# The first chunk's k is turned on TensorE instead of loaded; every piece is issued in a new order

## The chip, the cores and the metric

One core of a Trainium2 chip runs the whole program. The metric is the device time of one execution in microseconds (us), the median over several runs. Two versions of this kernel can be told apart by measurement when they differ by some 0.2%, which is about 0.4 us here.

## The reference

Attention with a per-head decay, in blocks of 64 positions with a running state, followed by a gated convolution layer. Sizes: 4 batches, 8 heads, 768 positions, head size 64, model width 512.

```python
for b in range(nb):                              # nb = 768 / 64
    intra = einsum('bhic,bhjc->bhij', qb, kb) * Dmask          # lam ** (i - j), lower triangle
    intra = einsum('bhij,bhjd->bhid', intra, vb)
    inter = einsum('bhid,bhde->bhie', qb * lam_pow, kv_state)
    out[:, :, sl] = intra + inter
    kb_dec = kb * rev_pow                                      # lam ** (63 - j), for each row of k
    kv_state = lam_block * kv_state + einsum('bhsd,bhse->bhde', kb_dec, vb)
# x = out as (batch, position, 512)
gate = sigmoid(causal convolution of x with 5 taps per column)
return (gate * (x @ w_val)) @ w_out
```

## The kernel before, in words

Two batches are worked on at a time (`b` = 0, 1), and their 768 positions are cut into six chunks of 128. That makes twelve chunks, numbered 0 to 11. Chunks 0, 1 and 2 are "big": their scores are 128x128 per head. The others use two blocks of 64. Every chunk has two loads on the sync engine's DMA queue (SP): `ld.i.0` brings q and k transposed (`qT`, `kT`, head size on the partitions, batch 0 on partitions 0 to 63 and batch 1 on 64 to 127), and `ld.i.2` brings v and k with positions on the partitions. Each load is 1024 KB. So k comes twice: `kT` serves the scores, k itself serves the state.

The work is cut into named pieces, each on one engine. For chunk i:

- `s.i.u` (TensorE, L460 for big chunks): scores of four heads from kT and qT. Matmuls of fp32 show up as two records each, so `s.0.0` is 8 matmuls and 16 records.
- `m.i.b.u` (VectorE, L483): scores times the decay mask, out of PSUM into the tile `A`.
- `ia.i.u` (TensorE, L525): A times v, into the PSUM tile `xp`. There is one such tile (`"xp": 1` in `SLOTS`, two banks), so every holder of it waits until all readers of the one before are done.
- `kd.i` (ScalarE L401 or GpSimd L404): k times the decay of each row, in place in the loaded tile. `K_ACT` lists the chunks for which ScalarE does it, with one instruction per head, 8 in all.
- `st.i` (TensorE, L564): the state's outer product of scaled k and v. `up.i.0` (VectorE) adds it to the state. `in.i.0` (TensorE, L536) is q times the state, with `qd.i.u` (GpSimd) having scaled q before.
- `x.i`, `xh.i`, `xl.i`: the chunk's result out of `xp`, as a whole (ScalarE, L634), and split in a high and a low part. For chunks 0 and 1 (`X_DVE`) `xh` (ScalarE, L664) and `xl` (VectorE, L672) read `xp` themselves.
- `v.i.f` (TensorE, L732): one quarter of x @ w_val from three products of high and low parts, 12 matmuls. `p.*` (TensorE, L841) is the product with w_out.
- `t.*` (convolution taps, one on ScalarE and four on VectorE), `sg.*`, `ap.*`, `hh.*`, `hl.*`: the gate and its product with the value.

The weights arrive as raw 64-bit floats (`wv.0`, `wv.1`, `wo.0`, `wo.1`, each 1024 KB) and are turned into high and low 32-bit parts in quarters: `e` and `n` (VectorE, L261 and L268), `r` and `m` (ScalarE, L273 and L278), `s`, `w`, `v` (VectorE, L281, L287, L293), `h` (ScalarE, L299) and `l` (GpSimd, L303).

At the start TensorE is warmed with nine matmuls of zeros (`WARM`, L188), and one more dummy matmul, `f.0` (L206), is placed by the order.

The order is written out by hand in the string `ORDER`: pieces are issued one after the other as listed, with the buffers they take behind a colon, and every engine works off its own pieces in that order. Synchronisation is added by the framework, which keeps engines apart by whole PSUM banks. Before the change, TensorE's pieces begin `s.0.0 s.0.1 ia.0.0 ia.0.1 f.0 st.0 s.1.0 s.1.1 v.0.0 ia.1.0 ia.1.1 in.1.0 st.1 s.2.0`, and VectorE's begin with the two mask-making pieces `dm.0 dm.1` (L216), then `m.0.0.0 m.0.1.0 m.0.0.1 m.0.1.1`, `e n` of the first quarter, `e` of the second, `s w v` of the first, `xl.0 up.0.0 m.1.1.0 m.1.0.0 m.1.0.1 m.1.1.1`.

Of the kernel before, what the change touches and what calls it, by code (L numbers as in the profile page):

```python
# [37 lines left out]
wv.0.1.w wv.0.1.v wv.0.1.h ld.3.2:lv1 wv.1.0.n s.2.0:s0 wv.1.1.e:val3 s.2.1:u1,u2 up.1.0 xh.1 wv.0.1.l v.0.1
m.2.0.0:A0 m.2.1.0 wv.1.0.m:u0 xl.1 wv.1.0.w wv.1.0.r hi.0 pb.0.0:val0 m.2.0.1:A1 wv.1.0.s cv.e qd.2.0:qd1 wv.1.0.v
qd.2.1 wv.1.1.n x.1 wv.1.1.r cv.r s.4.0:s0 cv.n v.1.0:u3 v.1.1 wv.1.0.h wv.1.1.s wv.1.1.m:u0 m.2.1.1 wv.1.1.w wv.1.1.v  # L40
ia.2.0:xp0 ia.2.1 wv.1.0.l cv.m m.4.1.0:A0 kd.2.0 wv.1.1.h fd.1.0 wo.0.0.n:val1 cv.s in.2.0 x.2:x1 pb.1.0:val2
wv.1.1.l m.4.0.0 st.2:u1 wo.0.0.e wo.0.0.r up.2.0 qd.4.0:qd0 cv.w cv.v xh.2:xs1 wo.1.1.e:val3 t.0.0.0:u2,g0 s.3.0:s0
xl.2.0 wo.0.0.m:u0 v.0.2:u3 m.3.0.0:A1 ld.6.2:lv2 v.0.3 pb.0.1 t.0.0.1 kd.3.0 t.0.0.2 xl.2.1 t.0.0.3 wo.0.0.w qd.4.1
ld.5.0:lq2 wo.0.0.s t.0.0.4 v.1.2:u1 sg.0.0 qd.3.1:qd1 v.1.3 v.2.2:u3 v.2.3 pb.1.1 wo.1.1.n fd.2.0 wo.0.0.v m.3.1.0
wo.1.1.m:u2 wo.1.1.r ld.6.0:lq0 st.3:u0,u1 wo.0.0.h qd.3.0 ia.3.0:xp0 in.3.0 wo.1.1.w wo.1.1.s wo.1.1.v wo.0.0.l hi.1
s.5.0:s0 kd.4.0 v.2.0:u2 up.3.0 in.3.1 wo.0.1.e:val1 wo.0.1.r fd.3.0 wo.1.1.h wo.0.1.n wo.0.1.m:u0 wo.0.1.s wo.1.1.l
up.3.1 fd.3.1 ia.3.1 v.2.1 x.3 xh.3 xl.3.1 ia.4.0:xp0 t.0.1.0:u1 ld.5.2:lv1 wo.0.1.w xl.3.0 pb.2.0:val3 m.5.1.0:A1
# [81 lines left out]
def decay_attention_then_gated_conv(  # L129
# [193 lines left out]

    def plan_load(i):
        pair, c = divmod(i, NC)
        lds[i] = {}
        for lo, tag in ((0, "lq"), (2, "lv")):
# [575 lines left out]
```

## Time and profile before

| what | us |
|---|---|
| median of 3 runs (206.31 to 206.44) | 206.38 |
| the profiled execution's own time | 206.52 |
| its span (first to last instruction) | 204.7 |
| VectorE busy | 154.1 (75%) |
| ScalarE busy | 114.3 (56%) |
| GpSimd busy | 115.4 (56%) |
| chain that ended last, share of TensorE | 87% |
| chain that ended last, share of DMA | 9% |

Times within a profile count from the span's start. A timeline row gives start, duration, engine, line, operation, output<-inputs, shape, and in brackets the idle time of the engine ahead of it and what ended that idle time. PE is TensorE's matmul stream, PEld its weight loads, DVE VectorE, ACT ScalarE, POOL GpSimd, SPq the issue of DMAs. A merged row of several instructions gives the time from the first start to the last end.

### The profile page before, as it was taken

What the parts mean: (1) busy time and instruction counts of PE and PEld (TensorE: products, weight loads), DVE (VectorE), ACT (ScalarE), POOL (GpSimd) and SP (SyncE); (2) the same over time, 40 slices, a digit from 0 to 9 for tenths busy, and PEclk for the clock granted to TensorE, in tenths of its full rate; (3) what the DMA queues carried; (4) which work ended last, traced back from release to release, by engine and by line L of the source; (5) the groups of instructions that cost most, each with busy time, mean ns of one, the idle gap of its engine ahead of it and who ended that gap; (6) DMA issues with size and microseconds to landing.
All of it is one profiled execution on the core that took longest, in us unless ns stands there. A gap on an engine that the chain in (4) does not pass through costs nothing.

```text
span 204.7 us, 7451 instructions
## 1 busy us (share of the span) xinstructions
PE 197.6 (97%) x3312; PEld 171.6 (84%) x3312; DVE 154.1 (75%) x240; ACT 114.3 (56%) x218; POOL 115.4 (56%) x113
## 2 busy tenths in 40 slices
PE   7789899999999999999999999999999999999994
PEld 7668899999899988899888888888878888888883
DVE  5778999998969987998979996582668499853200
ACT  2079589797975788646484665233636255423131
POOL 5446457897897499919919995893686100000000
PEclk9999999999999999999999999999999999999999
DMA  5999999981528004950890693004020002210232
GB/s 175 426 429 419 422 424 423 421 360 27 195 51 362 8 3 118 373 232 3 297 297 29 203 400 122 3 3 152 8 106 0 0 3 102 102 51 14 93 127 78
DMA packets 7952, 36.15 MB, mean 177 GB/s; under 512 B 1136, under 2 KB 1392, under 8 KB 4336
## 3 DMA queue, kind: packets, MB, share of 16 engines
q1 hardware_dynamic: 7920, 35.68, 45.2%
q8 instruction: 26, 0.43, 0.9%
q14 instruction: 6, 0.05, 0.1%
HBM read 29.38 MB, written 6.29 MB: 174 GB/s over the span
## 4 chain that ended last, share of the span: by engine, by line
PE 87%; DMA 9%; SPq 2%; issue 0%; ACT 0%; ACTq 0%
PE op L841 33%; PE vp L732 33%; DMA lq<-in_qkv 9%; PE xp L510 5%; PE s L470 5%; PE xp L547 5%; PE st L572 4%; SPq L337 1%; PE xp L525 1%; PE s L460 1%; PE st L564 1%; PE xp L536 1%; SPq L355 0%; PE so L460 0%; ACT o L848 0%
## 5 line engine op out<-in xcount | busy, mean ns | idle before, releaser
L706 DVE SCALAR_TENSOR_TENSOR acc<-x,conv_sb,acc 128x512 f32<-128x512 f32 x96 | 71.5, 753 | 7.8 <-ACT acc L704 5.7
L732 PE MATMUL vp<-x_hi,wv_hi 128*128 128x256 f32 (+1 forms) x144 | 47.1, 327 | 0.0
L732 PE MATMUL vp<-x_hi,wv_lo 128*128 128x256 f32 (+1 forms) x144 | 45.9, 319 | 0.3 <-POOL wv_lo L303 0.3
L732 PE MATMUL vp<-x_lo,wv_hi 128*128 128x256 f32 (+1 forms) x144 | 45.8, 318 | 0.0
L841 PE MATMUL op<-wo_hi,hs 128*128 128x512 f32 x96 | 30.4, 398 | 0.0
L848 ACT COPY o<-op 128x512 f32<-128x512 f32 (+1 forms) x25 | 14.3, 570 | 28.5 <-PE op L841 24.2
L732 PEld LDWEIGHTS vp<-x_hi,wv_hi 128*128 128x128 f32 x144 | 27.3, 190 | 2.8
L732 PEld LDWEIGHTS vp<-x_hi,wv_lo 128*128 128x128 f32 x144 | 27.4, 190 | 2.4 <-POOL wv_lo L303 0.5
L732 PEld LDWEIGHTS vp<-x_lo,wv_hi 128*128 128x128 f32 x144 | 27.4, 190 | 1.9
L677 POOL TENSOR_TENSOR x_lo<-x,x_hi 128x512 fp32r<-128x512 f32 x20 | 25.8, 1311 | 4.7 <-ACT x_hi L666 4.7
L584 POOL TENSOR_TENSOR sdec<-state,qdec_c 128x512 f32<-128x512 f32 x17 | 18.4, 1080 | 9.2 <-DVE state L581 9.2
L814 POOL TENSOR_TENSOR hs<-g,hs 128x512 fp32r<-128x512 f32 x12 | 15.4, 1294 | 13.6 <-ACT hs L803 13.6
L420 POOL TENSOR_TENSOR qd<-lq,qdec_c 128x512 f32<-128x512 f32 (+1 forms) x18 | 22.6, 1272 | 0.0
L841 PEld LDWEIGHTS op<-wo_hi,hs 128*128 128x128 f32 x96 | 17.7, 188 | 4.0
L841 PE MATMUL op<-wo_hi,h_hi 128*128 128x512 f32 (+1 forms) x52 | 20.0, 385 | 0.0
L841 PE MATMUL op<-wo_hi,h_lo 128*128 128x512 f32 (+1 forms) x52 | 19.6, 377 | 0.0
L704 ACT ACTIVATE acc<-x,conv_sb 128x512 f32<-128x512 f32 x24 | 16.7, 696 | 5.1 <-DVE state L581 3.6
L841 PE MATMUL op<-wo_lo,h_hi 128*128 128x512 f32 (+1 forms) x52 | 19.5, 375 | 0.0
L841 PE MATMUL op<-wo_lo,hs 128*128 128x512 f32 x48 | 18.9, 393 | 0.0
L803 ACT CAST h_hi<-vp 128x512 fp32r<-128x512 f32 x12 | 6.9, 587 | 21.0 <-DVE vp L778 21.0
L581 DVE TENSOR_TENSOR state<-st,sdec 128x512 f32<-128x512 f32 x17 | 11.7, 688 | 8.8 <-PE xp L547 6.4
L778 DVE TENSOR_TENSOR vp<-vp,g 128x512 f32<-128x512 f32 x12 | 8.3, 698 | 11.9 <-PE vp L732 11.9
(77 smaller groups left out, 356.8 us busy)
## 6 DMA issues: line engine op xcount, KB each, us to landing
lq<-in_qkv SPq DMA_DIRECT2D x12, 1024.0 KB, 7.8
lv<-in_qkv SPq DMA_DIRECT2D x12, 1024.0 KB, 8.0
out<-o SPq DMA_DIRECT2D x23, 256.0 KB, 2.5
w_raw<-in_w_val SPq DMA_DIRECT2D x2, 1024.0 KB, 12.6
w_raw<-in_w_out SPq DMA_DIRECT2D x2, 1024.0 KB, 17.6
out<-o SPq DMA_DIRECT2D x2, 128.0 KB, 1.8
conv_raw<-in_conv_w SPq DMA_DIRECT2D x1, 20.0 KB, 16.4
lam_bc<-in_lam SPq DMA_DIRECT2D x1, 4.0 KB, 1.6
```

Of the source, the lines that this page charges most:

```text
L420: nc.gpsimd.tensor_tensor(out=s["qd"][:, hs, ms], in0=lds[i]["qT"][:, u].rearrange("p h (m i) -> p h m i", m=2)[:, :, ms], in1=qdec[:, hs, ...
L470: nc.tensor.matmul(sp[b][rows(m), k, :], t["kT"][rows(b), u, h, ms], t["qT"][rows(b), u, h, ms], start=True, stop=True,)
L510: nc.tensor.matmul(s["xp"][rows(hh), b ^ m, b, g, :], lds[i]["v"][rows(m), b, h * D : (h + 1) * D], s["A"][rows(m), b, h, :], start=b == 0 ...
L581: nc.vector.tensor_tensor(out=state, in0=s["st"][m], in1=sdec, op=ALU.add)
L584: nc.gpsimd.tensor_tensor(out=sdec, in0=state, in1=qdec_c[:, :, n - 1 : n].to_broadcast([P, H, D]), op=ALU.mult)
L677: nc.gpsimd.tensor_tensor(out=s["x_lo"][:, ts], in0=s["x"][:, ts], in1=s["x_hi"][:, ts].bitcast(F32), op=ALU.subtract)
L704: nc.scalar.mul(to, src, w)
L706: nc.vector.scalar_tensor_tensor(out=to, in0=src, scalar=w, in1=to, op0=ALU.mult, op1=ALU.add)
L732: nc.tensor.matmul(to, w[:, ct, fs], xx[:, ct], start=n_mm == 0, stop=n_mm == 3 * NT - 1)
L814: (nc.vector if direct else nc.gpsimd).tensor_tensor(out=to, in0=x["h", j, fs], in1=x["to", j, fs].bitcast(F32), op=ALU.subtract)
L841: nc.tensor.matmul(s["op", b, j][:, cols], hh, w[:, ft, cols], start=ft == 0 and n == 0, stop=ft == NT - 1 and n == 2,)
L848: nc.scalar.copy(s["o", b, j][:, cols], s["op", b, j][:, cols])
```

## The change

For the chunks listed in `K_PE` (chunk 0 alone), `ld.0.2` brings v only, 512 KB. The host lays v and k out as two separate halves of the `lv` tile for this. A new TensorE piece, `tr.0`, multiplies `kT` of every head and batch with an identity of 64x64 (`eye`, made at the start by two small ScalarE copies): 16 matmuls with weights of 64x128 and 64 moving columns. The result, k with positions on the partitions, stands in the `xp` tile. `kd.0.0` moves from GpSimd to ScalarE, reads that PSUM tile and writes the scaled k into the empty half of the `lv` tile. `ORDER` is new from end to end.

```diff
-K_ACT = (1, 2, 3, 4, 6)
+K_ACT = (0, 1, 2, 3, 4, 6)
+K_PE = (0,)
 ORDER = """
-ld.0.0:lq0 dm.0 dm.1 qe ld.0.2:lv0 kd.0.0 s.0.0:s0 kd.0.1 m.0.0.0:A0 s.0.1:u0,u1 m.0.1.0 ia.0.0:xp0 wv.0:g0 ld.1.0:lq1
-ld.1.2:lv1 wv.1:g1 m.0.0.1:A1 m.0.1.1 ia.0.1 f.0:u2 wv.0.0.e:val0 ld.2.0:lq2 wv.0.0.n ld.4.0:lq0 cv wv.0.0.r
...
+dm.0 f.0:u0 ld.0.0:lq0 s.0.0:s0 ld.0.2:lv0 wv.0:g0 ld.1.0:lq1 ld.1.2:lv1 dm.1 m.0.0.0:A0 tr.0:xp0 s.0.1:u0,u1 m.0.1.0
+m.0.1.1:A1 wv.1:g1 m.0.0.1 kd.0.0 ld.2.0:lq2 ld.4.0:lq0 wv.0.0.n:val0 ld.2.2:lv2 cv wv.0.0.e wv.0.0.r wo.0:hs0
+wv.0.0.m:u2 wv.0.1.e:val1 wv.0.1.n wv.0.0.s ia.0.0:xp0 ia.0.1 wv.0.0.w wv.0.0.v xh.0:xs0 qe qd.1.0:qd0 wv.0.0.h
+st.0:u3 up.0.0 s.1.0:s0 wv.0.0.l s.1.1:u0,u1 xl.0 m.1.1.0:A0 m.1.0.1:A1 m.1.0.0 qd.1.1 v.0.0:u2 ld.3.0:lq1 m.1.1.1
+wv.0.1.m:u3 wv.0.1.w wo.1:hs1 fd.0.0 wv.0.1.r wv.0.1.s wv.1.1.e:val2 x.0:x0 wv.0.1.v ld.3.2:lv0 wv.1.0.n:val3
+ia.1.0:xp0 ia.1.1 in.1.0 wv.1.1.n wv.1.0.e kd.1.0 st.1:u0 wv.0.1.h wv.0.1.l x.1 xh.1 wv.1.1.r up.1.0 fd.1.0 s.2.0:s0
...
+    eye = const.tile([P, D], F32, name="eye")
+    for b in range(NB2):
+        nc.scalar.copy(eye[rows(b)], ident[rows(b), rows(b)])
...
-                if lo:
-                    lds[i].update(v=t[:, :, 0], k=t[:, :, 1])
...
+                    if lo:
+                        lds[i].update(v=t[:, 0], k=t[:, 1])
...
+            for part in ((0, 1),) if lo and i in K_PE else ((0, 2),):
+
+                def go(lo=lo, part=part, tile_of=tile_of, src=qkv[pair, c]):
+                    nc.sync.dma_start(tile_of()[:, slice(*part)], src[:, lo + part[0] : lo + part[1]])
...
+            if i in K_PE:
+                for h in range(H):
+                    nc.scalar.mul(kv[:, :, h], held[i]["kt"][:, :, h], k_mask[:, h])
+                return
...
+            def turn(i=i, s=s):
+                s["kt"] = bank("kt", [P, NB2, H, D], "xp")
+                for h in range(H):
+                    for b in range(NB2):
+                        nc.tensor.matmul(
+                            s["kt"][:, b, h], lds[i]["kT"][rows(b), h // HP, h % HP, :], eye[rows(b)],
+                            start=True, stop=True,
+                        )
+
+            t_turned = [add(f"tr.{i}", "PE", turn, [t_ld[i, 0], t_ld[i, 1]], [ld_buf[i, 0], *kt_bufs])]
...
-            [np.stack([heads(q), heads(k)], axis=4), np.stack([tokens(v), tokens(k)], axis=4)], axis=3
+            [np.stack([heads(q), heads(k)], axis=4), np.stack([tokens(v), tokens(k)], axis=3)], axis=3
```

After the change TensorE's pieces begin `f.0 s.0.0 tr.0 s.0.1 ia.0.0 ia.0.1 st.0 s.1.0 s.1.1 v.0.0 ia.1.0 ia.1.1 in.1.0 st.1 s.2.0`. VectorE's are, behind `dm.0 dm.1`: `m.0.0.0 m.0.1.0 m.0.1.1 m.0.0.1`, `n e` of the first quarter, `e n` of the second, `s w v` of the first, `up.0.0 xl.0 m.1.1.0 m.1.0.1 m.1.0.0 m.1.1.1`. ScalarE's begin `kd.0.0`, `r m` of the first quarter, `xh.0`, `h`, then `m r` of the second, `x.0 kd.1.0`.

## Rows read from the trace of the kernel before

**Rows 1.** The page's first part: engine, busy us, share of the span, instructions.
```profile
PE 197.6 (97%) x3312; PEld 171.6 (84%) x3312; DVE 154.1 (75%) x240; ACT 114.3 (56%) x218; POOL 115.4 (56%) x113
```
**Rows 2.** The chain that ended last: start, us, what.
```profile
4.34 18.07 DMA lq<-in_qkv
...
22.45 1.16 PE s L460 x16
...
48.81 0.62 PE xp L547 x32
49.43 0.47 PE xp L510 x32
```
**Rows 3.** Windows: stretch, length, busy PE PEld DVE ACT POOL, clock, DMA share, GB/s.
```profile
5.30:22.45 17.15, 14.28 (x238) 11.96 (x238) 13.75 (x25) 8.63 (x20) 7.81 (x7) 1.00 1.01 424
22.45:201.70 179.25, 179.12 (x3056) 155.71 (x3056) 137.37 (x208) 103.82 (x196) 104.61 (x93) 1.00 0.41 153
```
**Rows 4.** TensorE's timeline up to the state product of chunk 1.
```profile
1.05 4.21 PE L188 MATMUL warm<-zero 128*128 128x128 f32 x18 [1.05 <-DVE zero L179]
...
6.21 1.16 PE L460 MATMUL s<-lq 64*128 64x128 f32 x16 [0.95 <-DMA lq<-in_qkv]
7.20 1.06 PE L460 MATMUL so<-lq 64*128 64x128 f32 x16
8.78 2.06 PE L525 MATMUL xp<-A,lv 128*64 128x128 f32 x32 [0.51 <-DVE A L483]
10.76 1.12 PE L206 MATMUL fill<-zero 128*128 128x512 f32 x2
...
13.64 1.16 PE L460 MATMUL s<-lq 64*128 64x128 f32 x16 [0.45 <-DMA lq<-in_qkv]
...
17.85 1.97 PE L525 MATMUL xp<-A,lv 128*64 128x128 f32 x32
19.75 1.10 PE L536 MATMUL xp<-qd,state 64*64 64x128 f32 x32
20.78 1.15 PE L564 MATMUL st<-lv 128*64 128x64 f32 x32
```
**Rows 5.** VectorE's timeline in the same stretch.
```profile
7.42 1.29 DVE L483 TENSOR_TENSOR A<-s,mask_c 128x512 f32<-128x512 f32 x2 [0.93 <-PE s L460]
8.62 1.28 DVE L483 TENSOR_TENSOR A<-so,mask_c 128x512 f32<-128x512 f32 x2
...
11.16 0.43 DVE L261 TENSOR_SCALAR w_em<-w_raw 128x512 int32<-128x512 int32 x1 [1.26 <-DMA w_raw<-in_w_val]
11.51 0.42 DVE L268 TENSOR_SCALAR w_em<-w_raw 128x512 int32<-128x512 int32 x1
...
16.11 1.28 DVE L483 TENSOR_TENSOR A<-s,mask_c 128x512 f32<-128x512 f32 x2
...
17.31 1.28 DVE L483 TENSOR_TENSOR A<-so,mask_c 128x512 f32<-128x512 f32 x2
```
**Rows 6.** GpSimd's and ScalarE's timeline in the same stretch.
```profile
8.78 2.07 POOL L404 TENSOR_TENSOR lv<-lv,mask_c 128x512 f32<-128x512 f32 x2 [2.57 <-DVE A L483]
...
11.62 0.72 ACT L273 ACTIVATE w_em<-w_em,rebias 128x512 int32<-128x512 int32 x1 [9.40 <-DVE w_em L261]
...
15.14 1.27 POOL L303 TENSOR_TENSOR wv_lo<-w_em,wv_hi 128x512 fp32r<-128x512 f32 x1
...
17.71 2.45 ACT L401 ACTIVATE lv<-lv,mask_c 128x128 f32<-128x128 f32 x8 [0.42 <-DMA lv<-in_qkv]
```
**Rows 7.** Three lines' instructions: durations in ns (min/median/max), first and last start.
```profile
L460 PEld LDWEIGHTS s<-lq x48: 182/188/188, 6.2 to 23.2; 64*128 64x128 f32 x48
...
L564 PEld LDWEIGHTS st<-lv x96: 132/138/138, 12.0 to 34.0; 128*64 128x64 f32 x96
L564 PE MATMUL st<-lv x96: 222/222/271, 12.0 to 34.1; 128*64 128x64 f32 x96
...
L401 ACT ACTIVATE lv<-lv,mask_c x16: 384/386/401, 17.7 to 31.9; 128x128 f32<-128x128 f32 x16
```

More of the change, by code (lines that the diff above doesn't have):

```diff
@@ L38 @@
[L38 to L47, printed above, removed]
@@ L88 @@
+apw.5.0 hhw.5.0:hs0 o.9.1.0 apw.5.1 hhw.5.1 V.5.2:u1 hlw.5.0:val2 hlw.5.1 p.11.1.1.0:u0 p.11.0.0.0:u2 apw.5.3 hhw.5.3
+apw.5.2 hlw.5.3:val3 hhw.5.2 hlw.5.2 p.10.1.0.0:u3 p.11.1.1.1 ev.11.1.1:o2 o.11.1.1 o.8.0.0 p.10.1.0.1 ev.10.1.0:o0
+p.10.0.0.0:u1 p.10.0.0.1 ev.10.0.0:o2 p.11.0.0.1 o.10.1.0 ev.11.0.0:o1 p.11.1.0.0:u0 p.11.1.0.1 ev.11.1.0:o0 o.10.0.0
+o.11.0.0 o.11.1.0
 """
@@ L321, in decay_attention_then_gated_conv @@
     lds = {}
-    t_ld, ld_buf = {}, {}
+    t_ld, ld_buf, ld_tile = {}, {}, {}
     def plan_load(i):
@@ L328, in plan_load, with tile_of @@
             ld_buf[i, lo] = Buf(tag)
-            def go(i=i, lo=lo, tag=tag, src=qkv[pair, c]):
-                t = buf(tag, tag, [P, 2, 2, DM])
-                if lo:
-                    lds[i].update(v=t[:, :, 0], k=t[:, :, 1])
-                else:
-                    hd = t.rearrange("p a w (h i) -> p a w h i", h=HP)
-                    lds[i].update(qT=hd[:, :, 0], kT=hd[:, :, 1])
-                nc.sync.dma_start(t, src[:, lo : lo + 2])
-            t = add(f"ld.{i}.{lo}", "DMA", go, [], [ld_buf[i, lo]])
-            for part in range(lo, lo + 2):
-                t_ld[i, part] = t
+            def tile_of(i=i, lo=lo, tag=tag):
+                if (i, lo) not in ld_tile:
+                    t = ld_tile[i, lo] = buf(tag, tag, [P, 2, 2, DM])
+                    if lo:
+                        lds[i].update(v=t[:, 0], k=t[:, 1])
+                    else:
+                        hd = t.rearrange("p a w (h i) -> p a w h i", h=HP)
+                        lds[i].update(qT=hd[:, :, 0], kT=hd[:, :, 1])
+                return ld_tile[i, lo]
+            for part in ((0, 1),) if lo and i in K_PE else ((0, 2),):
+                def go(lo=lo, part=part, tile_of=tile_of, src=qkv[pair, c]):
+                    nc.sync.dma_start(tile_of()[:, slice(*part)], src[:, lo + part[0] : lo + part[1]])
+                t = add(f"ld.{i}.{lo + part[0]}", "DMA", go, [], [ld_buf[i, lo]])
+                for q in range(*part):
+                    t_ld[i, lo + q] = t
+            if lo and i in K_PE:
+                t_ld[i, 3] = t
     class Weight:
```

93 lines of the change are left out of this document (49 added, 44 removed).

## The prediction

> **What bounds the kernel now.** I read the page's first part first: TensorE is busy for 97% of the span [rows 1]. That alone says only that the few idle stretches are the place to look. The windows show where they are: from 22.45 to 201.70 us TensorE is busy for 179.12 of 179.25 us at a granted clock of 1.00, while from 5.30 to 22.45 it is busy for 14.28 of 17.15 us and the DMA engines are full (share 1.01, 424 GB/s) [rows 3]. The chain that ended last says the same: it runs through a load up to 22.41 us, and at 22.45 `s.2.0` starts; from there on it is TensorE's own work [rows 2]. So the end moves with the start of `s.2.0`, unless the new order adds idle time or work behind it. The same pieces stand ahead of `s.2.0` in both orders, with `tr.0` added, and the same 144 pieces from it on. Hence the question: what sets the start of `s.2.0` afterwards?
>
> Before, two limits lie close together there. The load lands at 22.41. But TensorE itself ends `st.1` at 20.78 + 1.15 = 21.93 [rows 4], so it waits only 0.52 us. And the work ahead of that hangs on VectorE: `ia.1.0` starts at 17.85 [rows 4], 0.46 us behind its two masks (16.11 + 1.28 = 17.39) [rows 5]. An earlier load is worth something only as far as this second limit moves too.
>
> **The change part by part, with its sum.**
>
> *The load.* `ld.0.2` gives up 512 KB. At 424 GB/s [rows 3] that is 1.24 us, and all later loads land that much earlier: `ld.2.0` at 21.17, `ld.1.0` at 12.4 instead of 13.6, and the first weights near 9.9 instead of 11.16, where VectorE now waits 1.26 us for them [rows 5]. This bounds any gain by 1.24 us.
>
> *k's scaling leaves GpSimd.* That frees 2.07 us at 8.78 [rows 6]. GpSimd's next work, `qd` and the first `l` (15.14), hangs on the next load and on ScalarE, so I count 0. ScalarE takes it in time that it had free: it sat idle for 9.40 us until 11.62 [rows 6]. The two `eye` copies fall in the same idle time: 0.
>
> *`f.0` goes ahead of `s.0.0`.* The warm-up ends at 1.05 + 4.21 = 5.26 and `s.0.0` starts at 6.21, after 0.95 us of idling for its load [rows 4]. `f.0` took 1.12 us at 10.76 [rows 4], part of which is run-out that overlaps its successor. Its 18 warm-up neighbours are 0.23 us apart, though, where `ia.0` handles the same 128 columns in 0.06 us a record, two halves side by side [rows 4]. [...] Between 0 and 0.6 us of delay; I take 0.1, as `s.0.0` at 6.21 already runs as fast as `s.1.0` at 13.64 [rows 4]. At its old place `f.0` cost nothing: TensorE waited 0.45 us for a load behind it.
>
> *`tr.0` itself.* 16 fp32 matmuls are 32 records, with weights of 64x128 and 64 moving columns. No row shows this shape. If the weights set the pace, it takes as long as `s.0.0` and `s.0.1` together, which are 32 records with the same weights: 7.20 + 1.06 − 6.21 = 2.05 us, or 1.8 without the last one's run-out [rows 4]. If the moving columns set the pace, the nearest row is `st.1`, 32 records of 64 moving columns: 1.15 us less 0.22 of run-out, 1.0 at most [rows 4, 7]. I take 1.8. A weight load of 128 columns takes 188 ns and one of 64 takes 138 [rows 7]: 50 ns more for 64 columns, so some 100 ns of loading for 128, and with two batches side by side some 50 ns a record. 32 of them are 1.6 us, far nearer to 1.8 than to 1.0.
>
> [...]
>
> *What waits for `tr.0`.* Two chains start behind it. On VectorE, the masks of `s.0.1` can't start before `s.0.1` is done: 7.20 + 1.06 + 0.1 + 1.8 = 10.16, instead of 8.62 [rows 4, 5]. Two masks take 1.28 (from start to start of the next pair 1.20), so the first weights begin at 11.45, though they have been there since 9.9. Before, they began at 11.16, when they arrived. From there to the first mask of chunk 1 VectorE needed 16.11 − 11.16 = 4.95 us; now one more `n` lies between (0.35, the distance of two such pieces) [rows 5], so the masks begin at 16.75. And the order of these masks is `m.1.1.0 m.1.0.1 m.1.0.0`: `ia.1.0` needs the third, not the second. It ends at 16.75 + 1.20 + 0.68 = 18.63. `ia.1.0` can start at 18.7, where it stood at 17.85. `ia.1`, `in.1` and `st.1` take 4.0 us (17.85 to 21.93 less the run-out of the last) [rows 4]. So `s.2.0` starts at 22.7: 0.25 us later than before, and 1.5 us behind its load. The gain of 1.24 us has been paid away.
>
> The second chain runs through the one `xp` tile. `ia.0.0` can't write it before ScalarE has read k out of it. `tr.0` ends at 9.15; eight scalings took 2.45 us in `kd.1.0` [rows 6], so ScalarE is done at 11.65, and `ia.0` starts at 11.7 instead of 8.78. It takes 2.0, `st.0` 1.1 [rows 4]: ready at 14.8. `up.0.0` is due on VectorE some 3.5 us behind the start of the first weights, at 14.95. The two chains meet almost to the point, with 0.15 us to spare. `s.1` follows on TensorE at 14.75 to 16.6, and `v.0.0` has its weights' low part about 17.0 (`l`: 1.27 us on GpSimd, 15.75 on [rows 6]), ending about 18.2, just ahead of the masks. What is queued behind `ia.0.0` on TensorE (`st.0`, `s.1`) has waited with it from 10.0 to 11.7. If `kd.0.0` takes longer out of PSUM, all of it moves. Its bounds are 2.45 and, without any overlap, 8 x 0.386 = 3.09 us [rows 6, 7]; I take 2.45, the same shape on the same engine.
>
> *Behind `s.2.0`.* Each change between small matmuls and 128x128 ones costs TensorE about 0.15 us (0.62 against 0.47 for the same 32 records) [rows 2]. I counted the runs in both orders: 20 of small pieces each. So the sum of TensorE's work there is the same. The old order left 0.13 us of idling in it [rows 3]; the new one can hardly gain, and can lose where its VectorE or ScalarE pieces come late. VectorE is busy for 137 of 179 us there [rows 3], so there is room on the whole: I take 0, with up to 0.5 of loss. The last pieces are again half an output row block of chunk 11 with its eviction and its 128 KB store: 0.
>
> *Sum.* +0.25 us on the profiled execution's 206.52. The median of the runs lies 0.14 below that execution, so 206.38 + 0.25 = 206.6.
>
> **The rivals.**
>
> A, *the turn is short* (moving columns set its pace). For it speaks that every other fp32 group here keeps the pace of its moving columns; against it that each of them has weights which load no slower. `tr.0` is 0.8 shorter, both chains move up, `s.2.0` starts at 21.9, 0.55 earlier than before and still behind its load: 205.8. If on top VectorE's chain shrank until the load alone decided, it would be 205.1.
>
> B, *the detour through `xp` decides, and the kernel is slower.* Place: `ia.0.0` behind `kd.0.0`. It decides once `kd.0.0` takes over 2.6 us (or starts 0.15 late). At 3.09 us `st.0`, `up.0.0` and with it `xl.0` and the masks of chunk 1 come 0.5 later: `s.2.0` at 23.2, 207.1. [...] For it: 0.15 us is thin. Against it: the scaling's 2.45 us is measured on the same shape.
>
> [...]
>
> D, *stalls later in the new order*, 0.5 us or more: about 207.1.
>
> **How the numbers follow.** Forecast 0.43, A 0.25, B 0.19, C 0.03, D 0.10. Two versions of this kernel can be told apart at about 0.2%, 0.41 us. The forecast's +0.25 is inside that, and I leave its own spread there, as A, B and D are what would carry it out. Faster 0.25 (A), same 0.43, slower 0.32 (B, C, D). The time is the forecast's, 206.6. The range goes from A's 205.8 to a little above B and D, 207.2. Of the forecast alone it would be 206.3 to 206.9.
>
> **What the profile after would show.** `tr.0`: 32 records on TensorE in 1.8 us (A: 1.0). `s.0.0` at 6.3. `kd.0.0` on ScalarE for 2.45 us and `ia.0` starting about 11.7, behind it (B: later than 12.2). VectorE's first weight piece at 11.45, waiting for nothing from the DMA. `ia.1.0` waiting for VectorE and starting at 18.7; `s.2.0` at 22.7, not waiting for its load. From there on TensorE busy without a gap. The prediction is wrong if `s.2.0` starts before 22.1 or after 23.1, or if more than 0.3 us of idling shows up behind it.

## The result and the profile after

The changed kernel took 208.46 us in the median of 15 runs (206.41 to 210.13), the kernel before 206.38 (206.19 to 206.73) on the same chip. The ratio is 1.008, with an interval of 1.006 to 1.0099: slower, and outside the range of the prediction (206.6, 205.8 to 207.2). Ratios leave out runs more than 1.5% above the fastest run of the same kernel.

The median hides how the time is made up. The runs of before lie within 0.6 us. Those of the changed kernel fall in groups: three at 206.41 to 206.56, eleven at 207.86 to 208.65, one at 210.13. So two questions have to be told apart: what the kernel costs when nothing goes wrong, and what goes wrong in most of its runs.

The profiled execution of after took 208.19 us. The page's first part, to set beside [rows 1]: TensorE has 1.4 us more work and as good as the same share.

```profile
PE 199.0 (96%) x3344; PEld 173.0 (84%) x3344; DVE 154.9 (75%) x240; ACT 118.1 (57%) x228; POOL 112.8 (55%) x111
```

TensorE's timeline of after up to `s.2.0`, to set beside [rows 4] (the quarter products of L762 are left out):

```profile
5.32 1.94 PE L210 MATMUL fill<-zero 128*128 128x512 f32 x2
7.19 1.16 PE L490 MATMUL s<-lq 64*128 64x128 f32 x16
8.18 1.90 PE L452 MATMUL kt<-eye,lq 64*128 64x64 f32 x32
9.92 1.11 PE L490 MATMUL so<-lq 64*128 64x128 f32 x16
12.36 1.97 PE L555 MATMUL xp<-A,lv 128*64 128x128 f32 x32 [1.33 <-ACT lv L413]
14.16 1.10 PE L594 MATMUL st<-lv 128*64 128x64 f32 x32
...
20.59 1.97 PE L555 MATMUL xp<-A,lv 128*64 128x128 f32 x32 [0.34 <-ACT lv L417]
...
24.61 1.16 PE L490 MATMUL s<-lq 64*128 64x128 f32 x16
```

`f.0` took 1.94 us where it took 1.12 before. That is about the warm-up's pace, 0.23 us for 128 columns [rows 4], at which its two records of 512 take 1.9 us (the slow pace below; 1.12 is the full pace). `s.0.0` starts at 7.19 instead of 6.21. (The column of granted clocks says 1.00 there, but the clock records of this trace begin only at 6.99 us, at 1.00, and say nothing of the time before.) The turn takes 1.74 us from its start to that of `s.0.1`. `s.2.0` starts at 24.61, 2.16 us later than before.

A second loss lies between `ia.0` and `ia.1`, which start 8.23 us apart (12.36 and 20.59) where the prediction had 7.0 (11.7 and 18.7). VectorE's and GpSimd's timelines of after at this place show it:

```profile
13.31 0.42 DVE L272 TENSOR_SCALAR w_em<-w_raw 128x512 int32<-128x512 int32 x1
13.85 1.56 DVE L285 SCALAR_TENSOR_TENSOR w_em<-w_raw,w_em 128x512 int32<-128x512 int32 x1
15.34 0.68 DVE L291 SCALAR_TENSOR_TENSOR w_v<-w_raw,w_v 128x512 f32<-128x512 uint32 x1
...
18.46 0.68 DVE L513 TENSOR_TENSOR A<-s,mask_c 128x512 f32<-128x512 f32 x1
```
```profile
13.45 1.42 POOL L429 TENSOR_TENSOR qd<-lq,qdec_c 128x512 f32<-128x512 f32 x1 [7.18 <-DMA lq<-in_qkv]
```

VectorE's `s` piece (L285) takes 1.56 us; undisturbed it takes 0.69 (a later profile, below). It started while GpSimd's `qd` was running and ended 0.54 us behind it. The 0.87 us go straight into the masks and `ia.1`. In the old order `qd` started at 13.73, when this piece was done (L281 there, 12.38 to 13.07).

The windows of after, then those of before, cut at the start of `s.2.0` and where 2,765 matmuls are left (in after the end of `s.3.0`):

```profile
0.00:24.61 24.61, 20.86 (x289) 17.94 (x289) 18.31 (x35) 13.04 (x32) 9.73 (x19) 1.00 0.90 362
24.61:38.20 13.59, 13.03 (x297) 11.98 (x293) 12.24 (x23) 12.02 (x28) 9.29 (x9) 1.00 1.02 425
38.20:203.35 165.15, 165.10 (x2765) 143.08 (x2764) 124.37 (x184) 92.71 (x169) 93.76 (x84) 1.00 0.34 124
```
```profile
22.45:35.39 12.94, 12.94 (x293) 12.00 (x293) 12.87 (x25) 11.27 (x27) 8.78 (x8) 1.00 1.02 424
35.39:201.70 166.31, 166.19 (x2765) 143.70 (x2764) 124.50 (x184) 92.55 (x171) 95.83 (x86) 1.00 0.36 132
```

In this execution the start costs 2.16 us, and the stretch up to the end of `s.3.0` 0.65 more (13.59 against 12.94), most of it a wait for a mask; behind it the same number of matmuls, 2,765, takes 1.16 us less. The sum, +1.65, is the difference of the executions but for 0.02 (208.19 against 206.52). The wait, from TensorE's timeline:

```profile
37.04 1.16 PE L500 MATMUL s<-lq 64*64 64x64 f32 x64 [0.56 <-DVE A L520]
```

### The profile page after: what moved, and what is told of

It is laid out like the page before. It is cut to its first block, busy times and chain, and to the rows that moved or that the text cites. A ratio compares the mean times of both kernels' runs of the same rounds, so it can differ in the third digit from the quotient of the medians.

```text
span 206.4 us, 7525 instructions
## 1 busy us (share of the span) xinstructions
PE 199.0 (96%) x3344; PEld 173.0 (84%) x3344; DVE 154.9 (75%) x240; ACT 118.1 (57%) x228; POOL 112.8 (55%) x111
## 4 chain that ended last, share of the span: by engine, by line
PE 90%; DVE 5%; ACT 3%; POOL 1%; issue 0%; ACTq 0%
PE op L871 33%; PE vp L762 31%; PE xp L577 5%; PE xp L540 5%; PE s L500 4%; PE st L602 4%; PE warm L189 2%; DVE w_em L285 1%; DVE A L513 1%; PE s L490 1%; PE so L490 1%; PE xp L555 1%; PE fill L210 1%; PE kt L452 1%; DVE w_em L297 1%; ACT w_em L277 1%
## 5 line engine op out<-in xcount | busy, mean ns | idle before, releaser
L762 PE MATMUL vp<-x_hi,wv_hi 128*128 128x256 f32 (+1 forms) x144 | 47.1, 327 | 0.2 <-ACT wv_hi L303 0.2
L762 PE MATMUL vp<-x_lo,wv_hi 128*128 128x256 f32 (+1 forms) x144 | 45.9, 319 | 0.8 <-DVE x_lo L702 0.8
L762 PE MATMUL vp<-x_hi,wv_lo 128*128 128x256 f32 (+1 forms) x144 | 45.9, 319 | 0.0
L762 PEld LDWEIGHTS vp<-x_hi,wv_hi 128*128 128x128 f32 x144 | 27.3, 190 | 3.4 <-ACT wv_hi L303 0.4
L762 PEld LDWEIGHTS vp<-x_lo,wv_hi 128*128 128x128 f32 x144 | 27.4, 190 | 2.9 <-DVE x_lo L702 1.0
L762 PEld LDWEIGHTS vp<-x_hi,wv_lo 128*128 128x128 f32 x144 | 27.4, 190 | 1.9
L741 ACT ACTIVATE g<-acc 128x512 f32<-128x512 f32 x24 | 14.2, 595 | 12.9 <-DVE acc L736 12.9
L871 PE MATMUL op<-wo_lo,hs 128*128 128x512 f32 x48 | 18.7, 390 | 0.0
L611 DVE TENSOR_TENSOR state<-st,sdec 128x512 f32<-128x512 f32 x17 | 11.7, 687 | 8.7 <-PE xp L577 4.5
L520 DVE TENSOR_TENSOR A<-s,dmask 128x512 f32<-128x512 f32 x18 | 12.0, 683 | 5.2 <-PE s L500 5.2
```

The lines of the kernel that those rows point to most:

```text
L520: nc.vector.tensor_tensor(out=s["A"][:, b, hs], in0=s["s", us][b], in1=dmask[:, hs], op=ALU.mult)
L611: nc.vector.tensor_tensor(out=state, in0=s["st"][m], in1=sdec, op=ALU.add)
L741: nc.scalar.activation(xu[un]["g"][:, ct].rearrange("p u (b i) -> p b u i", b=NB2), xu[un]["acc", ct].rearrange("p b (u i) -> p b u i", u= ...
L762: nc.tensor.matmul(to, w[:, ct, fs], xx[:, ct], start=n_mm == 0, stop=n_mm == 3 * NT - 1)
L871: nc.tensor.matmul(s["op", b, j][:, cols], hh, w[:, ft, cols], start=ft == 0 and n == 0, stop=ft == NT - 1 and n == 2,)
```

## The experiments

Line numbers are those of the changed kernel. "a" kernels start from after, "b" kernels from before. The first four were to tell apart: the start, that is `f.0` at the slow pace and L285 (theory 1); the turn and its detour; a fall of the clock (theory 3); and stalls that the new order makes itself behind `s.2.0` (theory 4).

**a_f0_gap**: `f.0` out of the front, into the gap behind `s.0.1`.

```diff
-dm.0 f.0:u0 ld.0.0:lq0
+dm.0 ld.0.0:lq0
...
-s.0.1:u0,u1 m.0.1.0
+s.0.1:u0,u1 f.0:u2 m.0.1.0
```

> The changed kernel with f.0 moved from ahead of s.0.0 to behind s.0.1, into the gap in which TensorE waits for ScalarE's kd.0.0; all else as it is. [...] Theory 2 (the turn and the detour of k through the xp tile cost the time whatever f.0 does): at most 1 us off, runs at 207.5 to 208.5.

Measured: 209.83 (206.45 to 211.24, 12 runs), ratio 1.0075 (1.0037 to 1.0113). The start is mended: `s.0.0` at 6.37, L285 0.69 us, `s.2.0` at 22.91. Yet where theory 1 had every run near 206.5, only two of the 12 took that (206.45 and 206.47), and the profiled execution took 208.55, because of something new on TensorE:

```profile
46.63 0.39 PE L762 MATMUL vp<-x_hi,wv_lo 128*128 128x256 f32 x1 [1.84 <-issue]
```

TensorE stopped for 1.84 us and waited for no semaphore, no engine and no data transfer that the profile shows ("issue").

**a_no_f0**: no `f.0` at all.

```diff
-FILL = 1
+FILL = 0
```

> The changed kernel without f.0. Theory 1: as with f.0 in the gap, near 206.5 us. If the two groups of runs come from TensorE's clock falling back in the idle stretch ahead of ia.0 (theory 3), this kernel idles longest there and shows the slow group more often than any other: 208 us and above, with granted clocks under 1.00.

Measured: 208.24 (207.58 to 210.32, 6 runs), 1.0114 (1.0076 to 1.0152). `s.2.0` at 22.94, and nearly the same stop: 1.61 us up to 46.65. It stands behind the same count of TensorE's records as in a_f0_gap (729 matmuls and 730 weight loads, 729 and 729 there). As the four records of `f.0` are missing here, that is two matmul records further on in the program.

**b_f0_first**: before, with `f.0` in front.

```diff
-ld.0.0:lq0 dm.0 dm.1 qe
+f.0:u0 ld.0.0:lq0 dm.0 dm.1 qe
...
-ia.0.1 f.0:u2 wv.0.0.e
+ia.0.1 wv.0.0.e
```

> The kernel before with f.0 moved to the front, ahead of s.0.0, and nothing else. Theory 1: s.0.0 starts up to 1 us late here too, but VectorE waits 1.26 us for the first weights behind its masks, which absorbs it: within 0.2 us of the kernel before (206.4). If f.0 at the front costs TensorE's path by itself, whatever the load: 207.4.

Measured: 206.30 (206.16 to 206.54, 11 runs), 0.9994 (0.9986 to 1.0003), the same time. In the profiled execution `f.0` took 1.12 us, the full pace, and TensorE waited 0.44 us for a load behind it. No profile of this kernel has an `f.0` at the slow pace, so what that would cost here is not shown.

**a_no_turn**: the new order with k loaded, `tr.0` dropped.

```diff
-K_PE = (0,)
+K_PE = ()
...
-m.0.0.0:A0 tr.0:xp0 s.0.1
+m.0.0.0:A0 s.0.1
```

> The changed kernel's order and its f.0 at the front, but k of chunk 0 is loaded again (1024 KB) and scaled by ScalarE in place; tr.0 is left out. Theory 1: no wait for the turn, VectorE is ready by 10.6 and waits for the weights until 11.16, so the late s.0.0 is hidden again: 206.4 to 206.7, one group of runs. Theory 4 (the new order stalls by itself, behind s.2.0): 207.5 or more.

Measured: 211.45 (211.12 to 211.89, 4 runs), 1.0243 (1.0228 to 1.0258). Without the turn the kernel is slower still. `s.2.0` starts at 23.24, and "issue" stops add up to 3.2 us: 1.04 up to 47.53, 0.11 near 75.1, 0.75 up to 134.12, 1.34 up to 145.00. At the last two the share of the DMA engines is 0.00 where TensorE stops (from 132 to 135 us and from 143 to 144; 0.69 from 144 to 145). So TensorE stops without the turn too, and theory 1 covers only the start. This kernel has 64 records fewer than after, so it does not price the turn by itself.

*Theory 5.* The page of after counts 26 transfers of 16 KB on the queue for instructions, and TensorE has 6,688 records: some 257 a transfer (in before 26 too, and 6,624 records: 255).

```profile
q8 instruction: 26, 0.43, 0.9%
```

The theory: TensorE takes its own instructions in pieces of some 256 over the DMA engines. If the next piece arrives too late, TensorE stops, and the place is given by the number of instructions from the start and by nothing else. In two kernels a change of the instruction count must move the places.

**b_n48**: before, with `f.0` replaced by 24 tiny matmuls in front and 24 in the gap where `f.0` was.

```diff
-    nc.tensor.matmul(
-        bank("fill", [P, 4, C]), zero, zero[:, None, :].to_broadcast([P, 4, C]), start=True, stop=True
-    )
+    t = bank("fill", [P, 4, C])
+    for j in range(24):
+        nc.tensor.matmul(t[:16, 0, :16], zero[:, :16], zero[:, :16], start=True, stop=True)
```

> The kernel before with f.0 replaced by the same 24 + 24 small matmuls. Nothing else moves. Theory 5: the fourth bound now falls into the dense stretch at 33 to 36 us (109 matmuls in 3 us, DMA full), so TensorE should come to stand without a releaser near 36 us for 0.3 to 2 us, at a record 256n+192, and the median is 206.7 to 209. Rival (the place in the instruction stream does not matter): the small matmuls lie in idle time of the start, median 206.2 to 206.6, no idle stretch without a releaser over 0.2 us.

Measured: 211.68 (209.81 to 216.67, 6 runs), 1.0219 (1.0171 to 1.0268). The order and the work of before, 94 matmul records and as many weight loads more, and 5 us slower. The start is 1.15 us later (`s.2.0` at 23.60), and TensorE stops three times (0.31, 0.62 and 1.38 us). The place near 36 us that the expectation named was wrong; it counted the added matmul records but not their weight loads, 94 in place of 188.

**a_n48**: the same 48 in a_f0_gap.

> The changed kernel with f.0 replaced by 24 small matmuls ahead of s.0.0 and 24 behind s.0.1 (16x16 tiles of zeros): 47 more matmuls, 94 more TensorE records, ahead of the same program. Theory 5: the bounds of the pieces of 256 instructions lie 94 records earlier in the program, so the idle stretch no longer stands at the same matmul; stretches of idle time without a releaser, if any are left, stand at records 256n+192 counted from the first, and the one at 44.8 us is gone; start up to 0.5 us later, median 206.4 to 208.5. Theory 4: idle stretch at the same matmul of the program as before, record 1472+94, and the median 209.8 or more.

Measured: 210.83 (210.54 to 211.87, 5 runs), 1.0227 (1.0207 to 1.0248). The stop near 44.8 us is gone; three others have come, 0.99 up to 75.25, 1.25 up to 134.87 and 1.42 up to 145.76. The time was worse than expected.

**b_turn**: the order of before with the turn alone.

```diff
-ld.0.2:lv0 kd.0.0 s.0.0:s0 kd.0.1 m.0.0.0:A0 s.0.1:u0,u1 m.0.1.0 ia.0.0:xp0
+ld.0.2:lv0 s.0.0:s0 m.0.0.0:A0 tr.0:xp0 s.0.1:u0,u1 m.0.1.0 kd.0.0 ia.0.0:xp0
```

> The order of before with the turn alone: k of chunk 0 turned by TensorE behind s.0.0, scaled by ScalarE in front of ia.0.0, f.0 where it was. If the turn itself costs what the sum said: s.2.0 0.2 to 0.6 us later than before's 22.45, median 206.4 to 207.0, as far as no stretch of missing instructions arises from the 64 added records. If the turn is what makes the changed kernel slow: 208 or more.

Measured: 212.94 (211.76 to 218.5, 5 runs), 1.0301 (1.028 to 1.0322). `s.2.0` at 23.45; stops of 1.68, 0.89 and 0.68 us. The "208 or more" that was to speak against the turn came about, but by stops that tiny matmuls of zeros bring about just as well (b_n48).

Windows from the span's start to each stop, of a_f0_gap, b_turn, b_n48 and a_n48 in this order (the first two counts are TensorE's matmuls and weight loads up to there):

```profile
0.00:44.80 44.80, 41.14 (x729) 37.53 (x729) 36.58 (x70) 31.61 (x74) 26.77 (x33) 1.00 0.95 387
```
```profile
0.00:55.83 55.83, 51.85 (x1113) 48.00 (x1114) 47.65 (x84) 40.77 (x95) 34.02 (x40) 1.00 0.84 332
0.00:70.13 70.13, 64.47 (x1368) 59.65 (x1368) 56.84 (x98) 48.27 (x110) 44.39 (x48) 0.98 0.75 293
0.00:153.10 153.10, 146.55 (x3023) 129.98 (x3024) 123.31 (x196) 95.76 (x192) 104.86 (x104) 0.99 0.56 210
```
```profile
0.00:47.60 47.60, 43.44 (x858) 40.46 (x859) 39.63 (x73) 31.36 (x72) 29.66 (x36) 1.00 0.93 377
0.00:55.50 55.50, 51.03 (x1113) 47.37 (x1114) 46.52 (x83) 37.18 (x82) 35.10 (x41) 1.00 0.85 340
0.00:75.78 75.78, 70.69 (x1623) 66.06 (x1623) 63.77 (x110) 51.50 (x111) 50.21 (x54) 1.00 0.71 280
```
```profile
0.00:74.25 74.25, 72.44 (x1623) 68.13 (x1623) 63.21 (x110) 54.09 (x120) 46.05 (x50) 1.00 0.71 279
0.00:133.60 133.60, 130.81 (x2641) 117.60 (x2641) 112.79 (x181) 88.25 (x178) 90.15 (x92) 1.00 0.59 227
0.00:144.30 144.30, 140.25 (x2896) 125.62 (x2896) 116.98 (x187) 91.18 (x184) 96.97 (x97) 1.00 0.55 212
```

The sums are 1458; 2227, 2736, 6047; 1717, 2227, 3246; 3246, 5282, 5792. In a_no_turn they are 1459, 2991, 5027 and 5537. Measured from 1458 they lie 1, 3, 5, 6, 7, 14, 15, 16, 17 and 18 times 255 records on, to within four records. The stops are at different matmuls in these programs, yet at counts of one series. That is what theory 5 expects; a wait for data would follow the matmul, not the count.

**a_ld6**: a_f0_gap with chunk 6's load of q and k some 15 us later. TensorE's order is untouched.

```diff
-ld.6.0:lq0
+ld.6.0:lq1
...
-ld.7.0:lq1
+ld.7.0:lq0
```

> The changed kernel with f.0 behind s.0.1, and the load of q and k of chunk 6 in the slot of chunk 3 (lq1) in place of that of chunk 4 (lq0), so that it is issued some 15 us later; the load of chunk 7 takes lq0. TensorE's order is untouched. Theory 5 (TensorE runs out of its own instructions near 44.8 us, because the piece that it asks for at about 41 us comes late beside the bulk loads): the stretch of loads ends about 2.4 us sooner, near 42 us (1 MB at 420 GB/s), the fifth piece starts by 42.3 us, the idle stretch at 44.8 us (1.84 us) is gone or under 0.3 us, and the median falls from 209.8 to 206.3 to 206.9. Theory 4 (a wait of the new order on another engine): TensorE's order and waits are the same there, so the idle stretch stays and the median with it. If chunk 6's load comes too late, TensorE waits at s.6.0 for a DMA, which the profile would name.

Measured: 208.02 (206.36 to 210.82, 12 runs), 1.0022 (0.9999 to 1.0044). The expected median, 206.3 to 206.9, did not come. The piece of instructions (the transfer on q8, as theory 5 reads it) does come sooner, at 41.1 us. No stop in this profile (206.37 us) nor in four more. Five runs took 206.36 to 206.50, but two 207.68 and 208.37 and five 210.44 to 210.82.

*Theory 6*: the time is that of an undisturbed run plus the delay of `s.2.0`, plus the stop, plus what TensorE loses where its clock falls behind a stop. Single executions were profiled to see what sets the groups apart.

**after_again** and **after_third**, the changed kernel itself:

> The changed kernel once more, to see which of its groups of times (206.4 to 206.6, 207.9 to 208.7, 210.1) a profile falls in and what sets them apart. Theory 6: near 206.5 f.0 runs at full clock (about 1.1 us), s.2.0 starts at 22.9 to 23.1 us and there is no idle stretch without a releaser; near 208.5 either f.0 lasts 1.6 to 1.9 us and s.2.0 starts at 24.2 to 24.7, or TensorE stands for 1 to 2 us at record 1472; near 210 such a stretch is followed by some 3 us at half clock. Rival: the groups have the same start and no such stretches, and the difference lies in durations of other engines.

> The changed kernel a third time, with the same expectations: the start, the stretch at record 1472 and the granted clock behind it add up to the group that the time falls in.

Measured 207.81 and 208.52. In the first, `f.0` took 1.51 us, L285 1.68 and `s.2.0` started at 24.29, with no stop. In the second, all of the start is as it should be, and TensorE stops later. Its timeline:

```profile
5.28 1.13 PE L210 MATMUL fill<-zero 128*128 128x512 f32 x2
6.45 1.16 PE L490 MATMUL s<-lq 64*128 64x128 f32 x16
...
11.61 1.97 PE L555 MATMUL xp<-A,lv 128*64 128x128 f32 x32 [1.32 <-ACT lv L413]
...
23.00 1.16 PE L490 MATMUL s<-lq 64*128 64x128 f32 x16
...
46.73 0.27 PE L762 MATMUL vp<-x_hi,wv_lo 128*128 128x256 f32 x1 [1.83 <-issue]
```

**a_f0_gap_b** and **a_f0_gap_c**, the kernel a_f0_gap twice more:

> The changed kernel with f.0 behind s.0.1, once more. Theory 6: a time near 206.5 has no idle stretch without a releaser; near 208.5 one of 1.5 to 2 us at record 1472; at 209.3 to 211.2 the same one and behind it 1.5 to 3.5 us of half clock. Rival for the last group: a second idle stretch, or one of 3 us and more, at full clock.

> The same kernel again, with the same expectations by the group that its time falls in.

Measured 206.44 and 210.05. Their starts agree to 0.06 us. In the shorter one the piece of instructions came at 41.1 us (the DMA view has one on the queue between 41 and 42) and TensorE ran through; in the other there is none in that microsecond, it came at 44.4, and TensorE stopped for 1.83 us. The DMA view has the same row of this queue for a_f0_gap_b from 41 to 42 us and for a_f0_gap_c from 44 to 45:

```profile
q8 instruction: 1, 0.02, 5.8%
```

The other traces agree. In all four executions with a stop near 45 us (a_f0_gap, a_f0_gap_c, a_no_f0, after_third) the transfer of this piece, the fifth in the trace, starts at 44.37 to 44.44 us. In the nine of this order that run through (after, after_again, a_f0_gap_b, a_qd, a_tr_late and a_ld6 with three repeats) it starts at 41.1 to 43.0, and in a_ld6_d, whose whole program is 4.3 us late, at 46.07.

In a_f0_gap_c the clock fell behind the stop. Its windows:

```profile
45.00:46.00 1.00, 0.00 (x0) 0.00 (x0) 1.00 (x3) 1.00 (x4) 0.00 (x0) 1.00 0.14 57
46.00:47.00 1.00, 0.33 (x2) 0.33 (x3) 0.78 (x2) 1.00 (x5) 0.00 (x0) 0.97 0.00 0
47.00:50.00 3.00, 3.00 (x71) 2.77 (x73) 0.00 (x0) 1.23 (x4) 0.00 (x0) 0.50 0.02 5
50.00:51.00 1.00, 1.00 (x46) 0.93 (x39) 0.12 (x1) 0.00 (x0) 0.00 (x0) 0.82 0.00 0
```

The granted clock is 0.50 for 3.4 us (0.06 + 3.00 + 0.36). The quarter products' matmuls (L762) start 0.21 us apart in it and 0.12 behind it. The cost is estimated as half of the 3.4, 1.7 us, as if TensorE did half its work in it. b_turn shows the same behind its first stop (0.50 from 59.1 to 62.5 us).

**a_ld6_again**, **a_ld6_c** and **a_ld6_d**, chunk 6's load later, and a fifth execution, a_ld6_e (206.45 us, `s.2.0` at 22.89, no stop):

> The kernel with chunk 6's load later, once more. Its times were 206.4 to 206.5 (half) and 207.7 to 210.8. Theory 6: if the time is near 206.4, no idle stretch; if near 210.6, an idle stretch of 1.5 to 2.3 us at a record 256n+192 and half clock for about 3 us behind it, which the granted clock of the profile shows. Theory 5 in its first form (bulk loads alone set it): no such stretch at record 1472 in any run of this kernel.

> The kernel with chunk 6's load later, a third time: near 206.5 no idle stretch; near 208 one; at 210.4 to 210.8 one of about 2 us at a record 256n+192 and 2 to 3.5 us of half clock behind it. If the loads alone decide when a piece of instructions comes, no idle stretch at record 1472 in this kernel, and a time near 210.6 has another cause.

> The kernel with chunk 6's load later, once more. If a run near 210.6 is caught: theory 6 expects an idle stretch of about 2 us, now at the next place where it can stand (a multiple of some 255 records from the one of the changed kernel), with 3.4 us of half clock behind it; if it stands at record 1472 itself with the DMA queues empty, the loads are not what delays the piece. Near 206.5: none, as in the three profiles so far.

Measured 206.55, 207.57 and 210.81. The second has a late start (`s.2.0` at 24.06), though no `f.0` stands ahead of `s.0.0`, and no stop: L285 took 1.60 us there. The last is not what was expected: no stop and nothing at record 1472. The whole opening ran at about the slow pace. TensorE's timeline of a_ld6_d:

```profile
6.38 2.08 PE L490 MATMUL s<-lq 64*128 64x128 f32 x16 [1.12 <-DMA lq<-in_qkv]
8.25 3.52 PE L452 MATMUL kt<-eye,lq 64*128 64x64 f32 x32
11.55 2.02 PE L490 MATMUL so<-lq 64*128 64x128 f32 x16
13.51 2.07 PE L210 MATMUL fill<-zero 128*128 128x512 f32 x2
15.51 2.79 PE L555 MATMUL xp<-A,lv 128*64 128x128 f32 x32
18.14 1.10 PE L594 MATMUL st<-lv 128*64 128x64 f32 x32
```

Each piece takes nearly twice its time up to some 17 us (`s.0.0` 2.08 against 1.16 in a_ld6_again, `tr.0` 3.52 against 1.90, `f.0` 2.07 against 1.13), and `s.2.0` starts at 27.24. The column of granted clocks says 1.00 there too, but the trace's clock records begin only at 17.24 us.

This bears on the timed runs. The stop with the fall takes a_f0_gap_c's mean granted clock to 0.990. The five runs of a_f0_gap at 210.47 to 211.24 and the five of a_ld6 at 210.44 to 210.82 have 0.997 to 1.000, and a_ld6_d has 0.999. So a stop with such a fall does not fit these ten; an opening at the slow pace would fit, but none of them was profiled.

**a_qd**: after with GpSimd's `qd.1.0` moved away from L285, to just ahead of `qd.1.1`.

```diff
-qe qd.1.0:qd0 wv.0.0.h
+qe wv.0.0.h
...
-m.1.0.0 qd.1.1
+m.1.0.0 qd.1.0:qd0 qd.1.1
```

> The changed kernel with qd.1.0 on GpSimd moved to just ahead of qd.1.1, behind the first weight's low half: it no longer lies beside VectorE's L285 near 13.5 us. f.0 stays at the front. If VectorE waits for GpSimd there: L285 takes 0.69 us in place of 1.56, and with f.0 at 1.5 to 1.9 us s.2.0 starts at 23.3 to 23.8 us in place of 24.3 to 24.6; the group of runs near 208.5 that has no idle stretch moves to 207.2 to 207.7. If not (the length of L285 has another cause): s.2.0 at 24.3 or later in such a run, and the groups stay.

Measured: 207.49 (206.97 to 208.49, 6 runs), 1.0053 (1.0032 to 1.0073). `f.0` took 2.06 us in the profile, L285 0.69, and `s.2.0` started at 23.85. So of the 1.6 us that after's profile loses against 23.00, L285 is about half, and `f.0` the rest. The runs moved as expected, most of them to 207.0 to 207.7.

**a_tr_late**: a_ld6 with `tr.0` and `f.0` behind `s.0.1`.

```diff
-m.0.0.0:A0 tr.0:xp0 s.0.1:u0,u1 f.0:u2 m.0.1.0
+m.0.0.0:A0 s.0.1:u0,u1 tr.0:xp0 f.0:u2 m.0.1.0
```

> The kernel with chunk 6's load later, and the turn behind s.0.1 in place of ahead of it, with f.0 behind the turn. The masks of chunk 0 start 1.7 us sooner (8.6 us), VectorE's first weight piece starts as soon as w_raw has landed (10.2 to 10.6 us by the load that is gone, in place of 11.49), k is scaled from 10.2 to 12.4 us and ia.0 starts near 12.4 us. If VectorE's chain bounds the start: third mask of m.1 and ia.1 0.8 to 1.2 us sooner, s.2.0 at 21.8 to 22.2 in place of 22.83, and the fastest runs at 205.3 to 205.7. If ia.0 bounds it: s.2.0 at 23 or later and 206.4 or more. Fetch theory: the runs still fall in groups, some with idle stretches at records 256n+192.

Measured: 207.56 (206.79 to 208.55, 6 runs), 1.0062 (1.0041 to 1.0083). `ia.0` starts at 12.47 and `s.2.0` at 23.37: the second reading, in which the detour of k through `xp` bounds the start of this kernel.

The profiled executions of the new order with at most one stop, together. "Sum" is 206.44 (a_f0_gap_b) plus the delay of `s.2.0` against 22.91, plus the stop, plus the estimated 1.7 for the fall of the clock:

| execution | `s.2.0` | stop | clock | sum | measured |
|---|---|---|---|---|---|
| after | 24.61 | 0 | – | 208.14 | 208.19 |
| after_again | 24.29 | 0 | – | 207.82 | 207.81 |
| after_third | 23.00 | 1.83 | – | 208.36 | 208.52 |
| a_f0_gap | 22.91 | 1.84 | – | 208.28 | 208.55 |
| a_f0_gap_c | 22.97 | 1.83 | 1.7 | 210.03 | 210.05 |
| a_no_f0 | 22.94 | 1.61 | – | 208.08 | 208.22 |
| a_ld6 | 22.83 | 0 | – | 206.36 | 206.37 |
| a_ld6_c | 24.06 | 0 | – | 207.59 | 207.57 |
| a_ld6_d | 27.24 | 0 | – | 210.77 | 210.81 |
| a_qd | 23.85 | 0 | – | 207.38 | 207.66 |

The sum agrees to 0.3 us (a_ld6_again, a_ld6_e and a_tr_late, not listed, to 0.03). It falls short for the four kernels that stop three or four times: a_no_turn, a_n48, b_n48 and b_turn took 0.6 to 1.5 us more than their start, stops and clock give (for the two "b" kernels, counted from before). Idle time understates these stops where it was tried: matched matmul by matmul with a_f0_gap_b, a_no_turn loses 4.2 us at its four places, where the idle time adds up to 3.2. That closes its sum to 0.2 us; the other three were not matched so.

No version here is faster than the kernel before: the best executions of the new order equal it.

## Why the prediction was wrong

- **The load stops being the limit: right.** None of the three profiles of the changed kernel has VectorE waiting for the first weights or `s.2.0` for its load. When the weights land is seen in a_tr_late alone, at 10.65 us: 0.5 us sooner than before, not the forecast 1.24, which did not matter.
- **`tr.0`, 1.8 us: right** (1.74 in after). Rival A is refuted: at the pace of `st.1`'s moving columns it would have been 1.0.
- **`kd.0.0`, 2.45 us: 2.17 to 2.18.** Out of PSUM it took a little less; rival B did not decide. `ia.0` started at 11.61 in after_third (forecast 11.7).
- **VectorE's chain: right where nothing disturbs it.** In after_third the masks of chunk 1 begin at 16.85 (16.75), `ia.1` at 18.99 (18.7), `s.2.0` at 23.00 (22.7). By the sum above such a start without a stop gives 206.5, and three runs of fifteen took 206.41 to 206.56, none of them profiled. So the forecast of 206.6 is about the time of the kernel when nothing goes wrong, and that is in part luck: in a_f0_gap_b `s.2.0` is 0.46 us later than before (forecast 0.25), and TensorE's way from there to its end is 0.55 us shorter (178.71 against 179.26 us; forecast 0).
- **`f.0` ahead of `s.0.0`, "Between 0 and 0.6 us of delay; I take 0.1": the first step that failed.** `s.0.0` was later by 0.24, 0.55 and 0.98 us in three profiles of the changed kernel (6.21 before). No run shows the 0.1, and the bound of 0.6, for which no run gives a ground, was too low. The term differs from run to run, as `f.0` takes 1.13, 1.51 or 1.94 us; the clock records, which start at 1.00, begin at 5.05, 6.13 and 6.99 us in the same order. The prediction's own rows gave more: at the warm-up's 0.23 us for 128 columns, `f.0`'s two records of 512 take some 1.9 us, which puts `s.0.0` at 7.1, 0.9 late.
- **L285 beside `qd`: a term put at nothing.** The prediction counted GpSimd's freed time as 0, but the new order put `qd` beside a VectorE piece, which took 0.9 and 1.0 us more in two of three profiles. With `f.0` it makes the whole late start there (24.61 and 24.29 against the forecast 22.7 and the prediction's own limit of 23.1), and with `qd` moved away it is gone (a_qd).
- **Behind `s.2.0`, "I take 0, with up to 0.5 of loss": the second step that failed**, in the third profile (after_third) and in a_f0_gap and a_no_f0, where the start is mended. In after, two small things there more than cancel (0.65 lost ahead of `s.3.0`, 1.16 gained behind it; where the gain comes from was not tried). What was not foreseen is a stop of 1.8 us that the profile puts down to "issue" and theory 5 to missing instructions, and a possible 1.7 us (estimated) from 3.4 us at a granted clock of 0.50 behind it. Rival D had the place but neither the mechanism nor the size. Rival C, the clock, had a chance of 0.03 for a fall in the idle stretch ahead of `ia.0`, and the three profiles of the changed kernel show none there: TensorE sits idle for 1.32 to 1.33 us ahead of `ia.0`, and the granted clock is 1.00.
- **Why most runs are longer.** In the profiles of the changed kernel and of its variants that keep the turn, the record count (but for `f.0`) and chunk 6's load, the start is late and there is no stop (after, after_again, a_qd), or the start is on time and TensorE stops (after_third, a_f0_gap, a_f0_gap_c, a_no_f0). Only a_f0_gap_b has neither. How the twelve longer runs of the changed kernel divide between the two was not measured; three profiles, two and one, are all there is.
- **What the trace of before could have told.** Its chain has one such stop, of 0.10 us, and the window up to it counts 1,971 records, which is 1458 and twice 255, to three records. The chain's row and the window:

```profile
53.14 0.10 issue
```
```profile
0.00:53.00 53.00, 49.03 (x985) 44.86 (x986) 45.70 (x82) 36.36 (x80) 34.01 (x40) 1.00 0.86 349
```

  By theory 5 that reads as if the old order was close to running dry at one place, and the new order moved other work to these places; the sum had no term for it.

What stays open: why the piece comes at 41.1 us in one execution of a_f0_gap and at 44.4 in the next. The six profiles with chunk 6's load later have no stop, which speaks for the bulk loads as the cause of the delay, but does not show it: a_f0_gap_b has none either, at the old place of that load. And a_no_turn stopped at 133 and 143 us with nothing on the DMA engines as the stops began (share 0.00); perhaps a fast stretch of small matmuls is enough there. Why the slow pace lasted to 17 us in a_ld6_d and never in the profiles of after is open too.

## What to carry to other kernels

Compare kernels whose TensorE runs through many small matmuls by several profiles, not by one, and look at the idle time that the profile calls "issue": added instructions move the places where it can stand, and a new order moves other work to them, so even dummy matmuls in idle time can cost microseconds (5 us in b_n48). When a sum of small terms comes out near no change, list first the terms that differ from run to run: here TensorE's pace at the start (up to 0.98 us), a VectorE piece beside a GpSimd piece (0.9 to 1.0) and the stops that theory 5 puts down to the arrival of instructions (1.6 to 1.84) were each larger than the forecast difference of 0.25.

## What the runs showed of the hardware

- **TensorE stopped at counts of one series, and near 45 us only where a transfer of instructions came late.** All stops lie a multiple of 255 records apart, to within four, and where the transfer of the fifth piece started at 44.4 us instead of 41.1 to 43.0, TensorE stopped. The distance agrees with the records for each transfer on the queue for instructions (257 in after, 255 in before). That these transfers bring TensorE's instructions is read from the queue's name and these counts. The stops took 0.1 to 1.84 us each, and 3.7 us in one execution (a_n48).
- **A VectorE and a GpSimd instruction made each other longer.** In after, GpSimd's `qd` began first (13.45) and L285 took 1.56 us; in after_third L285 began first, took 0.69, and `qd` took 1.64 instead of 1.30:

```profile
13.12 0.69 DVE L285 SCALAR_TENSOR_TENSOR w_em<-w_raw,w_em 128x512 int32<-128x512 int32 x1
```
```profile
13.31 1.64 POOL L429 TENSOR_TENSOR qd<-lq,qdec_c 128x512 f32<-128x512 f32 x1 [7.11 <-DMA lq<-in_qkv]
```

  It does not hold for every VectorE instruction: the masks (L513), which read their scores from PSUM, took their usual 0.68 us at 19.06 and 19.66 in after, while another `qd` ran (18.71 to 20.01). Why one pair does and another does not was not shown. A small difference in the start went with a large one behind it: `s.0.0` starts at 6.47 in a_ld6_again and at 6.60 in a_ld6_c, where L285 takes 1.60 us beside a `qd` that began first (13.04 against 13.27); `ia.1` starts 7.36 and 8.29 us behind `ia.0`, and `s.2.0` at 23.02 and 24.06.
- **A stop can cost twice.** Behind the same stop of 1.83 us the granted clock fell to 0.50 for 3.4 us in a_f0_gap_c and stayed at 1.00 in after_third.
